# Loads of q, k and v issued in half-step portions behind TensorE's matmuls in a windowed-attention and mixture-of-experts kernel

## The chip, the cores and the metric

The kernel runs on one core of a Trainium2 chip. The metric is device time in microseconds (us) from the start to the end of one execution. The kernel before takes 690.67 us, the median of three runs that lie between 690.36 and 690.69.

The engines are named as the profile names them: PE is TensorE (matmuls), PEld its weight loads, DVE is VectorE, ACT is ScalarE, POOL is GpSimd, and SP is SyncE, which does no arithmetic here and issues transfers (DMAs). "SPq" is SP's instruction queue as the profile shows it. Each engine works through its own instructions in the order in which they were written; engines wait for each other and for transfers by semaphores.

## The reference

Two stages are chained. The first is an attention over 8 batches and 8 heads, with 512 local positions, 32 global positions and a head dimension of 64. The second is a mixture of experts (MoE) in which each token takes one of 8 experts, and may keep the expert of the token ahead of it.

```python
k_all = np.concatenate([k_g, k_l], axis=2)
v_all = np.concatenate([v_g, v_l], axis=2)
out_g = np.matmul(sm(scale * q_g @ k_all.T), v_all)          # global rows see all
mask = np.abs(pos[:, None] - pos[None, :]) <= 32             # local rows: a window
s_ll = np.where(mask, scale * q_l @ k_l.T, -1e9)
a_l = sm(np.concatenate([scale * q_l @ k_g.T, s_ll], axis=-1))
out_l = np.matmul(a_l, np.concatenate([v_g, v_l], axis=2))
x = concatenate([out_g, out_l]) as rows of 512, one per token (8 x 576)
...
logits = x @ w_gate;  local_gate = sigmoid(x @ w_local)
e = argmax(logits) if s == 0 or local_gate < 0.5 else prev_e  # sticky top-1
out = softmax(logits)[e] * (relu(x @ w1[e]) @ w2[e])
```

All of it is float32. The `.T` and `@` above shorten the reference's own `matmul` and `transpose` calls.

## The kernel before

**Stages.** The first third of the time is the attention (class `Attn`), the rest is the MoE. The change touches the attention alone, with the transfers that feed it and the one that takes its rows away.

**Units and steps.** Each batch has six units, in the order l0, l1, g0, l2, g1, l3. An l unit is a pair of heads for the local rows, a g unit is two pairs for the global rows. `run` goes over the 48 units in steps; step s belongs to batch b = s // 6 and has the place k = s % 6 in it. A step does the first part of its own unit (scores and the row maximum) and the second part (transposes, product with v, division) of the unit two steps earlier. An l unit is done in two halves, hb 0 and hb 1, of eight windows each.

In one step of an l unit PE therefore runs: transposes of the unit two steps back (`l_t`, L260), scores of the first half (`l_s`, mask L238 and products L243), one piece of a list of small follow-up work (`fpiece`), the product with v for the first half (`l_av`, L276), scores of the second half, another piece, and `l_av` of the second half. A step of a g unit runs `g_s` (L296) in place of the scores.

**The follow-up pieces** compute the gate for a batch that has ended: `f1` (L352, transposes of the batch's rows), `f1g`, `f2g` (L375), `f2` (L367, the gate's product) and `f3`. After `f3`, a generator `f3k` computes routing keys and probabilities on DVE in small portions (`drip`, called at fixed places between the other work), and ends with `f4`, the batch's store. So the store of batch b is written out during step k = 2 of batch b + 2, behind the DVE instruction at L771, which is the last to write into the rows.

**Buffers.** `raw` holds q and k of a pair, in a ring of four (528 KB each); `v` is a ring of five (1040 KB each); `qgb` a ring of two. A batch's output rows stand in `xa`, a ring of two (1056 KB each; 128 partitions by 4 row groups by 528 columns), and its global rows in `xg`, also a ring of two. Half hb of an l unit writes row groups 2 hb and 2 hb + 1 of `xa` (L284). Since the ring has two places, the first L284 of batch b + 2 can only write when the store of batch b has landed. In PSUM, `ps_s` has four banks for scores, `ps_t` two for transposes, and `ps_o` two, which `l_av`, `g_av`, `f2` and parts of `f3` take in turn: each needs the reader of the bank's earlier content to be done. The reader of an `l_av` bank is that half's chain on DVE, which ends with L284.

**Order.** The program is written under a manual schedule: each engine's queue holds the instructions in the order in which the Python code emits them. All loads and stores of this stage stand in SP's one queue, so that a DMA on SP which waits for a semaphore holds up every DMA behind it there. Besides its data waits, each DMA on SP waits for one of eight lanes (named DMAHW0 to DMAHW7 in the listing), that is for the landing of the DMA eight places ahead of it.

**Loads before the change.** At the head of each l step, `run` issues the qk load two pairs ahead (`load`, L178), with the global q at a batch's first pair (L182), and the v load one pair ahead (`loadv`, L188, one transfer of 1040 KB). The row store (L413) is one transfer of 1056 KB, followed by four small stores of the global rows (L417) and one of 32 rows of 16 columns (L418).

## Time and profile before

| What | Value |
|---|---|
| Median of three runs | 690.67 us (690.36 to 690.69) |
| The profiled execution | 694.06 us |
| Its span, first to last instruction | 692.3 us |
| PE busy | 670.5 us, 97% of the span |
| DVE busy | 426.2 us, 62% |
| ACT busy | 342.9 us, 50% |
| POOL busy | 207.7 us, 30% |
| Mean granted TensorE clock | 0.995 |
| Moved by DMA | 151.44 MB, mean 219 GB/s |

The profiled execution takes 1.76 us more than its span (694.06 - 692.3), which lies ahead of the first and behind the last instruction, and 3.39 us more than the median of the timed runs (694.06 - 690.67).

The profile is of one execution. Times in it count from the start of the span. A row of the timeline has the start, the time from there to the end of the last of a run of like instructions, the engine, the line, the operation, the output tile and the input tiles, and a count; in brackets stands the idle time of that engine just ahead of it, and what released it. A row of the waits has who waited for whom: the sum, the number of times, the longest. A row of the windows has the length of the stretch, then the busy time of PE, PEld, DVE, ACT and POOL with their instruction counts, the granted clock, the busy share of the DMA engines and what they moved in GB/s. Line numbers are those of the kernel before; those of the changed kernel are some 20 higher.

### The profile page before, as it was taken

The numbers are of one execution on the slowest core, as the hardware profiler recorded it, in microseconds if no ns is written. First come the engines' busy times: TensorE is split into PE (matmuls) and PEld (weight loads), VectorE is DVE, ScalarE is ACT, GpSimd is POOL, SyncE is SP. The second block draws the span as 40 slices with busy tenths as digits, with TensorE's granted clock in tenths as the row PEclk, the third lists the DMA queues.
The fourth block names the chain that finished last, engine by engine and source line by source line (L and its number), as shares of the span: only waits on it lengthen the run. The fifth ranks groups of instructions, "written<-read, shape, count | busy, mean of one in ns | idle before, by whom it ended". The sixth has DMA issues, their size and how long they took to land.

```text
span 692.3 us, 18408 instructions
## 1 busy us (share of the span) xinstructions
PE 670.5 (97%) x7253; PEld 561.1 (81%) x7253; DVE 426.2 (62%) x1050; ACT 342.9 (50%) x614; POOL 207.7 (30%) x342
## 2 busy tenths in 40 slices
PE   9999999999989899998998999999999999999995
PEld 7777777777767787897887988889898889888994
DVE  7878677688887777995517535335354516255572
ACT  4555556555455674653326625344444325255553
POOL 7634334343674301033013303040404020133023
PEclk9999999999999999999999999999999999999999
DMA  8956957866856497777418647337475417265673
GB/s 318 405 220 233 346 193 309 310 248 231 299 196 273 147 356 243 260 243 245 174 60 308 232 149 239 102 117 235 145 225 191 140 61 231 66 222 193 212 270 103
DMA packets 43011, 151.44 MB, mean 219 GB/s; under 512 B 7965, under 2 KB 9245, under 8 KB 38688
## 3 DMA queue, kind: packets, MB, share of 16 engines
q1 hardware_dynamic: 35536, 126.92, 51.6%
q0 software_dynamic: 6960, 21.90, 9.5%
q8 instruction: 77, 1.26, 0.7%
q14 instruction: 150, 1.23, 0.6%
q10 hardware_dynamic: 288, 0.13, 0.1%
HBM read 130.55 MB, written 19.69 MB: 217 GB/s over the span
## 4 chain that ended last, share of the span: by engine, by line
PE 60%; DVE 3%; issue 1%; ACT 0%; POOL 0%; POOLq 0%; DVEq 0%; ACTq 0%
PE ps L1267 29%; PE ps L1256 27%; PE ps L1210 3%; DVE wq L1165 1%; DVE wp L1165 1%; PE ps L1004 0%; PE ps L1379 0%; DVE xl L1165 0%; DVE xT L994 0%; POOL xa L1196 0%; DVE xT L996 0%; POOLq L1427 0%; DVE wp L1213 0%; PE ps L276 0%; DVE wq L1371 0%
## 5 line engine op out<-in xcount | busy, mean ns | idle before, releaser
L1273 POOL DMA_INDIRECT out_dram<-y,tk x39 | 40.4, 1036 | 317.6 <-ACT y L1272 246.3
L1267 PE MATMUL ps<-wp,wq 128*128 128x512 f32 x504 | 128.4, 402 | 1.0 <-ACT wq L1370 1.0
L1267 PEld LDWEIGHTS ps<-wp,wq 128*128 128x128 f32 x504 | 93.5, 190 | 21.1 <-ACT wq L1370 1.2
L1256 PE MATMUL ps<-wp,wp 128*128 128x256 f32 (+5 forms) x672 | 109.3, 322 | 0.2 <-issue 0.2
L1256 PEld LDWEIGHTS ps<-wp,wp 128*128 128x128 f32 x672 | 103.6, 188 | 5.3 <-issue 0.4
L1259 DVE SCALAR_TENSOR_TENSOR wq<-ps,wq 128x256 fp32r<-128x256 f32 (+5 forms) x80 | 41.7, 525 | 72.8 <-ACT wq L1258 62.6
L1213 DVE TENSOR_TENSOR wp<-ps,wp 128x512 fp32r<-128x512 f32 x40 | 27.5, 691 | 78.9 <-ACT wp L1212 78.8
L1258 ACT ACTIVATE wq<-ps 128x256 fp32r<-128x256 f32 (+5 forms) x80 | 37.3, 468 | 78.3 <-PE ps L1256 68.8
L191 POOL TENSOR_SCALAR_AFFINE_SELECT qbd<-raw 64x512 f32<-64x512 f32 x62 | 44.4, 716 | 103.3 <-PE ps L243 85.5
L243 PE MATMUL ps<-kx,qbd 128*64 128x128 f32 x1024 | 71.3, 280 | 0.2 <-issue 0.2
L1272 ACT ACTIVATE y<-ps,pp 128x512 f32<-128x512 f32 x39 | 26.9, 690 | 77.7 <-PE ps L1267 71.1
L243 PEld LDWEIGHTS ps<-kx,qbd 128*64 128x64 f32 x1024 | 55.1, 137 | 12.2 <-issue 7.8
L248 DVE TENSOR_REDUCE mx<-ps 128x4 f32<-128x512 f32 x64 | 43.9, 687 | 29.9 <-PE ps L243 29.9
L1165 DVE TENSOR_TENSOR wp<-raw,wp 128x1024 fp32r<-128x1024 f32 x47 | 57.0, 1217 | 2.8 <-ACT wp L1155 2.8
L254 ACT ACTIVATE pe<-pe 128x512 f32<-128x512 f32 x64 | 40.7, 637 | 31.7 <-DVE pe L250 31.7
L1196 POOL DMA_INDIRECT xa<-xs,idx x42 | 50.9, 1212 | 17.1 <-issue 9.4
L1155 ACT CAST wp<-raw 128x1024 fp32r<-128x1024 f32 x49 | 50.8, 1047 | 0.8 <-ACT hh L1258 0.5
L1212 ACT CAST wp<-ps 128x512 fp32r<-128x512 f32 x40 | 23.4, 590 | 53.9 <-PE ps L1210 53.3
L250 DVE TENSOR_TENSOR pe<-ps,mx 128x512 f32<-128x512 f32 x64 | 44.0, 688 | 1.6
L276 PEld LDWEIGHTS ps<-v,pt 128*32 128x32 f32 x2048 | 33.4, 110 | 13.1 <-issue 7.3
L276 PE MATMUL ps<-v,pt 128*32 128x65 f32 x2048 | 42.8, 222 | 1.1 <-issue 0.4
L262 ACT COPY pt<-ps 128x512 f32<-128x512 f32 x64 | 34.9, 610 | 17.6 <-PE ps L260 17.6
(280 smaller groups left out, 1183.3 us busy)
## 6 DMA issues: line engine op xcount, KB each, us to landing
raw<-in_w_dram SPq DMA_DIRECT2D x78, 512.0 KB, 4.1
v<-in_vw_dram SPq DMA_DIRECT2D x32, 1040.0 KB, 9.8
raw<-in_qk_dram SPq DMA_DIRECT2D x32, 528.0 KB, 8.2
xa<-in_w_dram SPq DMA_DIRECT2D x26, 512.0 KB, 5.2
xT<-in_w_dram SPq DMA_DIRECT2D x20, 512.0 KB, 3.5
xs<-xa SPq DMA_DIRECT2D x8, 1056.0 KB, 4.9
qgb<-in_qg_dram SPq DMA_DIRECT2D x8, 128.0 KB, 3.5
xa<-xs,idx POOLq DMA_INDIRECT x42
```

The source lines that it names most:

```text
L191: self.nc.gpsimd.affine_select(out=out, in_=in_, pattern=pat, compare_op=ALU.is_ge, fill=0.0, base=0, channel_multiplier=0)
L243: nc.tensor.matmul(sp[64 * t2:64 * t2 + 64, t], qbd[:, w], kf[:, f:f + P], start=False, stop=True, skip_group_check=True)
L248: nc.vector.tensor_reduce(out=mx, in_=st["sp"], axis=AX.X, op=ALU.max)
L250: nc.vector.tensor_tensor(out=st["pe"][:, 4 * hb:4 * hb + 4], in0=st["sp"], in1=mx.broadcast_to([P, 4, P]), op=ALU.subtract)
L254: self.nc.scalar.activation(out=pe, in_=pe, func=AF.Exp, scale=SCALE)
L276: nc.tensor.matmul(o[32 * w4:32 * w4 + 32, g, h], pt[:, 2 * g + w4 // 2, w4 % 2, h, :], v[:, w, h * (D + 1):(h + 1) * (D + 1)], start=True ...
L1155: nc.scalar.copy(out=hi, in_=raw)
L1165: (nc.gpsimd if pool else nc.vector).tensor_tensor(out=lo, in0=raw, in1=hi.bitcast(F32), op=ALU.subtract)
L1196: self.nc.gpsimd.indirect_dma_start(out=self.xr[j] if k == "early" else self.xr4[:, j], out_offset=None, in_=src, in_offset=bass.IndirectO ...
L1256: nc.tensor.matmul(ph, a[:, dc, fs], b_[:, dc, n0:n1], start=(n == 0), stop=(n == 11))
L1259: nc.vector.scalar_tensor_tensor(out=hl[:, fc, n0:n1], in0=ph, scalar=0.0, in1=hh[:, fc, n0:n1].bitcast(F32), op0=ALU.max, op1=ALU.subtract)
L1267: nc.tensor.matmul(py, a[:, fc, js], b_[:, fs], start=(fc == 0 and k == 0), stop=(fc == 7 and k == 2))
```

## The change

Three things are changed, all in `Attn`.

1. **A gate on each load.** `l_s`, `l_av`, `g_s` and `g_av` keep their last matmul in `self.gate`. Every load of q, k and v goes through the new function `get`, which adds to the DMA a dependency on the matmul that stands in `self.gate` when the load is written out. The loads ahead of the first step have none.
2. **v in two halves, and another place for the loads.** `loadv` has a parameter `hf` and moves 8 of a pair's 16 windows (520 KB). The loads no longer stand at the head of an l step: the new function `feed(s, hf)` is called twice in every step, once behind the scores (hf 0) and once at the step's end (hf 1). With k = 0, 1, 2 it issues the two halves of the v of pair 1 + k of this batch; with k = 3 qk of pair 0 of the next batch with the global q, then qk of pair 1; with k = 4 the halves of the next batch's v of pair 0; with k = 5 qk of pairs 2 and 3. In the first batch it also issues qk of pairs 2 and 3.
3. **The row store in two DMAs**, of row groups 0 and 1 and of 2 and 3 (528 KB each).

The diff:

```diff
--- before.py
+++ after.py
@@ -132,6 +132,7 @@
         self.low = 0
         self.banks = False
         self.npr = 0
+        self.gate = None
 
     def make_mask(self):
         nc, m0 = self.nc, self.m0
@@ -169,23 +170,45 @@
         yield
         nc.sync.dma_start(self.xs[0:P], zr)
 
+    def get(self, out, in_):
+        d = self.nc.sync.dma_start(out, in_)
+        if self.gate is not None:
+            self.tc.add_manual_dep(d.ins, self.gate.ins.name, mybir.DependencyInfo(mybir.DependencyClass.Sync, mybir.DependencyReason.DATA), reason="pace")
+
     def load(self, b, pr):
-        nc = self.nc
         if pr == 0:
             self.cur[b] = {"v": []}
         c = self.cur[b]
         t = c[("qk", pr)] = self.ld()
-        nc.sync.dma_start(t, self.qk[b, pr])
+        self.get(t, self.qk[b, pr])
 
     def load_g(self, b):
         g = self.cur[b]["qg"] = self.qgb()
-        self.nc.sync.dma_start(g, self.qg[b])
-
-    def loadv(self, b, pr):
-        nc = self.nc
-        v = self.v()
-        self.cur[b]["v"].append(v)
-        nc.sync.dma_start(v.rearrange("p w c -> p (w c)"), self.vw[b, pr])
+        self.get(g, self.qg[b])
+
+    def loadv(self, b, pr, hf):
+        vs = self.cur[b]["v"]
+        if hf == 0:
+            vs.append(self.v())
+        n = NW // 2 * VW
+        self.get(vs[pr].rearrange("p w c -> p (w c)")[:, n * hf:n * hf + n], self.vw[b, pr][:, n * hf:n * hf + n])
+
+    def feed(self, s, hf):
+        b, k = divmod(s, 6)
+        if k < 3:
+            if b == 0 and k < 2 and hf == 0:
+                self.load(0, 2 + k)
+            self.loadv(b, 1 + k, hf)
+            return
+        b += 1
+        if b == B:
+            return
+        if k == 4:
+            self.loadv(b, 0, hf)
+        else:
+            self.load(b, (k - 3) + hf)
+            if (k, hf) == (3, 0):
+                self.load_g(b)
 
     def cp(self, out, in_, pat):
         self.nc.gpsimd.affine_select(out=out, in_=in_, pattern=pat, compare_op=ALU.is_ge, fill=0.0, base=0, channel_multiplier=0)
@@ -240,7 +263,7 @@
             for t2 in range(2):
                 w = 8 * hb + 2 * t + t2
                 f = 32 * (3 * (w // 2) + w % 2)
-                nc.tensor.matmul(sp[64 * t2:64 * t2 + 64, t], qbd[:, w], kf[:, f:f + P], start=False, stop=True, skip_group_check=True)
+                self.gate = nc.tensor.matmul(sp[64 * t2:64 * t2 + 64, t], qbd[:, w], kf[:, f:f + P], start=False, stop=True, skip_group_check=True)
 
     def l_max(self, st, hb):
         nc = self.nc
@@ -273,7 +296,7 @@
             for h in range(2):
                 for w4 in range(4):
                     w = 8 * hb + 4 * g + w4
-                    nc.tensor.matmul(o[32 * w4:32 * w4 + 32, g, h], pt[:, 2 * g + w4 // 2, w4 % 2, h, :],
+                    self.gate = nc.tensor.matmul(o[32 * w4:32 * w4 + 32, g, h], pt[:, 2 * g + w4 // 2, w4 % 2, h, :],
                                      v[:, w, h * (D + 1):(h + 1) * (D + 1)], start=True, stop=True, skip_group_check=True)
         rs = self.rs()
         nc.vector.tensor_scalar(out=rs, in0=o[:, :, :, D:D + 1], scalar1=1e-9, scalar2=None, op0=ALU.add)
@@ -293,7 +316,7 @@
             for i in range(2):
                 pr = 2 * pp + i
                 k = c[("qk", pr)][:, SL:]
-                nc.tensor.matmul(sp[64 * i:64 * i + 64, 0:n1 - n0], c["qg"][:, pr], k[:, n0:n1], start=True, stop=True, skip_group_check=True)
+                self.gate = nc.tensor.matmul(sp[64 * i:64 * i + 64, 0:n1 - n0], c["qg"][:, pr], k[:, n0:n1], start=True, stop=True, skip_group_check=True)
             st["sp"].append(sp[:, 0:n1 - n0])
 
     def g_max(self, st):
@@ -336,7 +359,7 @@
         for ci, w in enumerate(GCH):
             for i in range(4):
                 pr, h = 2 * pp + i // 2, i % 2
-                nc.tensor.matmul(op[32 * i:32 * i + 32, 0:D + 1], st["pt"][:, ci, 32 * i:32 * i + 32],
+                self.gate = nc.tensor.matmul(op[32 * i:32 * i + 32, 0:D + 1], st["pt"][:, ci, 32 * i:32 * i + 32],
                                  c["v"][pr][:, w, h * (D + 1):(h + 1) * (D + 1)], start=(ci == 0), stop=(ci == 5), skip_group_check=True)
         rs = self.rsg()
         nc.vector.tensor_scalar(out=rs, in0=op[:, D:D + 1], scalar1=1e-9, scalar2=None, op0=ALU.add)
@@ -410,7 +433,8 @@
         hf, b4 = b // 4, b % 4
         rq = slice(32 * b4, 32 * b4 + 32)
         r0 = P * (1 + col(b))
-        nc.sync.dma_start(self.xs[r0:r0 + 4 * P].rearrange("(t p) r -> p t r", p=P), xa)
+        for t in range(0, 4, 2):
+            nc.sync.dma_start(self.xs[r0 + t * P:r0 + t * P + 2 * P].rearrange("(t p) r -> p t r", p=P), xa[:, t:t + 2])
         r0 = P * (1 + gcol(hf)) + 32 * b4
         xsg = self.xs[r0:r0 + 32]
         for h in range(4):
@@ -437,7 +461,8 @@
         for k in range(2):
             self.load(*pairs[k]["u"])
         self.load_g(0)
-        self.loadv(*pairs[0]["u"])
+        for hf in range(2):
+            self.loadv(0, 0, hf)
         self.cst.ident()
         warm = self.ps_o()[:, 0:P]
         for _ in range(8):
@@ -456,13 +481,6 @@
             sl = st is not None and st["k"] == "l"
             sg = st is not None and not sl
             if nl:
-                if npr + 2 < len(pairs):
-                    b, i = pairs[npr + 2]["u"]
-                    self.load(b, i)
-                    if i == 0:
-                        self.load_g(b)
-                if npr + 1 < len(pairs):
-                    self.loadv(*pairs[npr + 1]["u"])
                 npr += 1
                 if npr < len(pairs):
                     self.prep(pairs[npr])
@@ -480,6 +498,7 @@
             else:
                 self.g_s(nx)
                 self.g_max(nx)
+            self.feed(s, 0)
             fpiece()
             if sl:
                 self.l_av(st, 0)
@@ -494,6 +513,7 @@
                 self.l_av(st, 1)
             if sg:
                 self.g_av(st)
+            self.feed(s, 1)
             if nl:
                 if s in DEFER:
                     late = nx
```

The instructions on PE, DVE, ACT and POOL stand in the same order as before. What moves is SP's queue, and some waits. The piece of SP's queue around the store of batch 1, before the change; `raw`, `v` and `qgb` are loads, `xs<-xa` is the row store, `xs<-xg` and `xs<-gx` are the small stores, and a wait on PE_49 or DVE_49 is on an instruction of that engine:

```order
L178 DMA raw_80<-in_qk_dram 128x1056 [waits DMAHW2_49,Pool_49]
L188 DMA v_136<-in_vw_dram 128x2080 [waits DMAHW3_49,PE_49]
L413 DMA xs<-xa_109 128x4x528 [waits DMAHW4_49,DVE_49]
L417 DMA xs<-xg_111 32x2x64 [waits DMAHW5_49]
L417 DMA xs<-xg_111 32x2x64 [waits DMAHW6_49]
L417 DMA xs<-xg_111 32x2x64 [waits DMAHW7_49]
L417 DMA xs<-xg_111 32x2x64 [waits DMAHW0_49]
L418 DMA xs<-gx 32x16 [waits DMAHW1_49,DVE_49]
L178 DMA raw_77<-in_qk_dram 128x1056 [waits DMAHW2_49,PE_49,Pool_49]
L182 DMA qgb_152<-in_qg_dram 128x256 [waits DMAHW3_49]
L188 DMA v_132<-in_vw_dram 128x2080 [waits DMAHW4_49]
```

The same piece after the change (L174 is every load, L437 the row store, L441 and L442 the small stores):

```order
L174 DMA v_136<-in_vw_dram 128x1040 [waits DMAHW2_49,PE_49]
L174 DMA v_136<-in_vw_dram 128x1040 [waits DMAHW3_49,PE_49]
L174 DMA v_132<-in_vw_dram 128x1040 [waits DMAHW4_49,PE_49]
L437 DMA xs<-xa_109 128x2x528 [waits DMAHW5_49,DVE_49]
L437 DMA xs<-xa_109 128x2x528 [waits DMAHW6_49]
L441 DMA xs<-xg_111 32x2x64 [waits DMAHW7_49]
L441 DMA xs<-xg_111 32x2x64 [waits DMAHW0_49]
L441 DMA xs<-xg_111 32x2x64 [waits DMAHW1_49]
L441 DMA xs<-xg_111 32x2x64 [waits DMAHW2_49]
L442 DMA xs<-gx 32x16 [waits DMAHW3_49,DVE_49]
L174 DMA v_132<-in_vw_dram 128x1040 [waits DMAHW4_49,PE_49]
L174 DMA raw_77<-in_qk_dram 128x1056 [waits DMAHW5_49,PE_49,Pool_49]
```

The first half of the next pair's v (`v_132`) now stands ahead of the row store. It is written out by `feed(s, 0)` of step k = 2, so its wait on PE is for the last matmul of that step's `g_s`; before, the whole `v_132` stood behind the store.

On DVE, the first two writes of a batch into its `xa` buffer, the two halves of unit l0, before; L279 and L281 form the divisor and L284 writes the rows:

```order
L279 TENSOR_SCALAR rs1_122<-ps7_70 128x4 [waits PE_49]
L281 RECIPROCAL rs1_122<-rs1_122 128x4 [waits DVE_49]
L284 TENSOR_TENSOR xa0_108<-ps7_70,rs1_122 128x2x128 [waits DMAHW5_49,DVE_49]
L279 TENSOR_SCALAR rs2_123<-ps6_69 128x4 [waits PE_49]
L281 RECIPROCAL rs2_123<-rs2_123 128x4 [waits DVE_49]
L284 TENSOR_TENSOR xa0_108<-ps6_69,rs2_123 128x2x128 [waits DVE_49]
```

And after:

```order
L302 TENSOR_SCALAR rs1_122<-ps7_70 128x4 [waits PE_49]
L304 RECIPROCAL rs1_122<-rs1_122 128x4 [waits DVE_49]
L307 TENSOR_TENSOR xa0_108<-ps7_70,rs1_122 128x2x128 [waits DMAHW1_49,DVE_49]
L302 TENSOR_SCALAR rs2_123<-ps6_69 128x4 [waits PE_49]
L304 RECIPROCAL rs2_123<-rs2_123 128x4 [waits DVE_49]
L307 TENSOR_TENSOR xa0_108<-ps6_69,rs2_123 128x2x128 [waits DMAHW2_49,DVE_49]
```

Before, only the first of the two writes waits for a DMA, the whole store; now the first waits for one store and the second for the other.

## Prediction

> **What bounds the kernel now.** I read the page's busy times first, then the windows of the attention stage by batches, then the timeline of single steps, and last the waits of SP's queue.
>
> ```profile
> PE 670.5 (97%) x7253; PEld 561.1 (81%) x7253; DVE 426.2 (62%) x1050; ACT 342.9 (50%) x614; POOL 207.7 (30%) x342
> ```
>
> PE is busy for 97% of the span. For the stage that is changed, the windows from one batch's start to the next (at PE's L359, which comes once in a batch) say more:
>
> ```profile
> 34.30:62.59 28.29, 28.11 (x590) 21.27 (x588) 21.22 (x75) 16.03 (x38) 11.06 (x25) 1.00 0.63 237
> 62.59:90.89 28.30, 27.89 (x589) 21.29 (x587) 21.30 (x72) 16.01 (x38) 11.06 (x25) 1.00 0.75 275
> 90.89:118.67 27.78, 27.78 (x589) 21.18 (x587) 21.13 (x72) 16.00 (x38) 11.05 (x25) 1.00 0.76 281
> 118.67:146.45 27.78, 27.78 (x589) 21.16 (x587) 21.15 (x72) 16.01 (x38) 11.06 (x25) 1.00 0.77 280
> ```
>
> Two of the four batches take 27.78 us and PE is busy for all of it, at full granted clock; DVE, the next, has 21. Loads and stores cost these two batches nothing. The other two take 0.51 and 0.52 more (28.29 - 27.78, 28.30 - 27.78). The two places:
>
> ```profile
> 36.08 0.87 PE L243 MATMUL ps<-kx,qbd 128*64 128x128 f32 x11 [0.17 <-issue]
> 84.05 0.27 PE L276 MATMUL ps<-v,pt 128*32 128x65 f32 x2 [0.41 <-issue]
> ```
>
> Both are "issue": PE waited for nothing that the profile shows. So smoother loading has at most 1.03 us to win here, and that only if these gaps have to do with DMA traffic. With PE full, whatever now makes PE wait in a batch is added to the end.
>
> **What the change removes, adds and moves.** *The splits.* 32 v loads become 64 and 8 row stores become 16, 40 more DMAs on SP. An issue costs SP some 0.4 us (rows at 91.77 and 96.21 below), so 5 more per batch are 2 us of SP's time; SP does nothing else, and in the piece of timeline below it is idle for most of a batch. Price 0; it would count only where something urgent stands behind them, which is the next point. *The gates on PE.* A gate needs a signal from a matmul that PE executes anyway, and eight more separate semaphore instructions; the like of them stand in the trace:
>
> ```profile
> L359 PEldq EVENT_SEMAPHORE  x7: 51/51/51, 33.7 to 208.2; - x7
> ```
>
> Eight by 0.051 is 0.41 us at most; PEld has 6 us of room in a batch, so I take 0.
>
> *The row store.* This is the term that I forecast by. SP before, around the store of batch 1:
>
> ```profile
> 91.77 0.38 SPq L413 DMA_DIRECT2D xs<-xa  x1
> 92.19 3.91 SPq L417 DMA_DIRECT2D xs<-xg  x4
> 96.21 0.37 SPq L418 DMA_DIRECT2D xs<-gx  x1
> 96.71 1.44 SPq L178 DMA_DIRECT2D raw<-in_qk_dram  x1
> ```
>
> The store is issued right behind what it waits for, the last write of the rows:
>
> ```profile
> 91.66 0.08 DVE L771 MEMSET xa<- 128x28 f32 x1
> SPq L413 <- DVE xa L771: 48.0, 5, 11.3
> ```
>
> After the change a half of the next v stands ahead of it in the queue, and waits for the last matmul of `g_s` in step k = 2 (L296). The timeline of PE and DVE over the same time:
>
> ```profile
> 94.61 1.14 PE L296 MATMUL ps<-raw,qgb 128*64 128x256 f32 x8
> 95.67 0.27 PE L375 MATMUL ps<-xgT,wgg 128*32 128x32 f32 x8
> 97.33 0.42 DVE L284 TENSOR_TENSOR xa<-ps,rs 128x256 f32<-128x256 f32 x1 [0.42 <-DMA xs<-xa]
> 98.07 0.42 DVE L284 TENSOR_TENSOR xa<-ps,rs 128x256 f32<-128x256 f32 x1
> 99.67 1.06 PE L367 MATMUL ps<-xT,wgl 128*32 128x512 f32 x8
> 100.55 0.64 PE L276 MATMUL ps<-v,pt 128*32 128x65 f32 x32
> ```
>
> L296 is over at about 95.7. The v half then takes SP to about 96.2, and the first half of the store is issued there, the second at 96.65: 4.4 us and 4.9 us later than 91.77. Who waits for it: DVE's first L284 of batch b + 2 already now waits 0.42 us for the store's landing (in the store after that 1.12, below). After the change the first L284 waits for store half 0 and the second for half 1. Behind L284 on DVE stand the maxima of the next scores, and behind DVE stands PE: `f2` (L367, at 99.67) needs the PSUM bank that the first L284 reads, and the next `l_av` (L276, at 100.55) the bank of the second. Before, these two L284 end at 97.75 and 98.49, so PE has about 2 us of cover. The second L284 may start no later than 100.13 (100.55 - 0.42); what it starts later, PE loses.
>
> How long the landing takes. The waits of DVE give it for two stores: 97.33 - 91.77 = 5.56 us, and for the store at 119.55 the row below gives 125.81 - 119.55 = 6.26. The other two, at 63.46 and 147.33, were not waited for, so took less than 5.17 (68.63 - 63.46; 152.50 - 147.33).
>
> ```profile
> 63.46 0.38 SPq L413 DMA_DIRECT2D xs<-xa  x1
> 68.63 0.42 DVE L284 TENSOR_TENSOR xa<-ps,rs 128x256 f32<-128x256 f32 x1
> 119.55 0.38 SPq L413 DMA_DIRECT2D xs<-xa  x1
> 125.81 0.42 DVE L284 TENSOR_TENSOR xa<-ps,rs 128x256 f32<-128x256 f32 x1 [1.12 <-DMA xs<-xa]
> 147.33 0.38 SPq L413 DMA_DIRECT2D xs<-xa  x1
> 152.50 0.42 DVE L284 TENSOR_TENSOR xa<-ps,rs 128x256 f32<-128x256 f32 x1
> DMA to landing us min/median/max: 4.7/4.9/6.7
> ```
>
> The last row is that of L413, all eight. I take 5.2, between the median 4.9 and 5.56, for both halves together: they move the same bytes. Ahead of them now stands the v half, 520 KB (0.53 MB). At the rate of a stretch in which loads run alone and the DMA engines are full, it is 0.53 MB / 386 GB/s = 1.4 us:
>
> ```profile
> 104.00:106.00 2.00, 2.00 (x18) 1.25 (x17) 1.92 (x10) 1.39 (x3) 1.34 (x5) 1.00 1.01 386
> ```
>
> The store is issued 0.45 behind the v half, so it is pushed by 1.4 - 0.45 = 0.95 if the transfers are served in turn. No row shows that; the bounds are 0 and 1.4, and I take 0.95 because both go over the same 16 engines. [...]
>
> So the second half lands at 96.2 + 5.2 + 0.95 = 102.35, L284 ends at 102.77, and PE starts L276 at 102.77 instead of 100.55: **2.2 us** per batch. It falls on batches b + 2 = 2 to 5, four times, where the store is issued ahead of the gate. That of batch 4 is issued later in its batch, at 166.39, where the last gate ahead of it in the new order, the first half's scores in that step, has opened at about 165.5; the ones behind it lie likewise, so I charge them nothing.
>
> ```profile
> 164.50 1.09 PE L243 MATMUL ps<-kx,qbd 128*64 128x128 f32 x16
> 166.39 0.38 SPq L413 DMA_DIRECT2D xs<-xa  x1
> ```
>
> Sum: 4 x 2.22 = 8.9; less 1.03 for the issue gaps, which I take as gone since the loads in lumps go: +7.8 (rounded). The profiled execution took 694.06 (692.3 span and 1.76 around it), so 701.9; that execution is 3.39 above the median of the runs, so the forecast for the median is 690.67 + 7.8 = **698.5**.
>
> Its bounds: low, a landing of 4.7 and nothing for the v half: 96.2 + 4.7 + 0.42 - 100.55 = 0.77, by four 3.1, less 1.03: 692.7. High, 6.26 and 1.4: 3.73, by four 14.9, the gaps staying: 705.6.
>
> *The loads.* They are issued later: qk of the next batch's pair 0 waits for its gate (99.67), but stands behind the four small stores, 3.9 us, which now begin near 97.1; so at about 101.9, where before it was 96.71. The cover:
>
> ```profile
> 102.52 1.50 POOL L191 TENSOR_SCALAR_AFFINE_SELECT qbd<-raw 64x512 f32<-64x512 f32 x2 [6.48 <-PE ps L243]
> 104.08 1.33 POOL L191 TENSOR_SCALAR_AFFINE_SELECT kx<-raw 128x128 f32<-128x128 f32 x4
> 112.81 0.88 PE L243 MATMUL ps<-kx,qbd 128*64 128x128 f32 x12
> raw<-in_qk_dram SPq DMA_DIRECT2D x32, 528.0 KB, 8.2
> v<-in_vw_dram SPq DMA_DIRECT2D x32, 1040.0 KB, 9.8
> ```
>
> POOL rearranges it at 102.52, before PE uses it at 112.81 (115.0 with the delay). Even with the old median landing of 8.2 it is there at 110.1, and POOL's 2.9 us end at 113.0: POOL waits, PE does not. The v halves have two steps from gate to use, and a step is 27.78 / 6 = 4.6 us. So 0; if the cover were gone, each microsecond would be one of PE.
>
> At the end of the stage SP's first weight loads of the MoE stand behind the last gated loads, some 3 us later:
>
> ```profile
> 213.63 26.11 SPq L1145 DMA_DIRECT2D raw<-in_w_dram  x6
> 227.57 1.05 ACT L1155 CAST wp<-raw 128x1024 fp32r<-128x1024 f32 x1
> ```
>
> ACT uses the first 13.9 us after its issue, so 3 us less cost nothing.
>
> **Rivals.** *1. The store lands in time, faster.* A half of the store is half the bytes. The least time that a small store took, 1.5 us (row below), plus half of what the whole takes beyond it, (4.9 - 1.5) / 2 = 1.7, is 3.2 us; if the halves and the v half are served side by side, half 1 lands at 96.65 + 3.2 = 99.85, ahead of 100.13, and PE waits for nothing. If the issue gaps then go with the lumps in the loads, it is 690.67 - 1.03 = **689.6**. It decides from a landing of half 1 within 3.48 us of its issue.
>
> ```profile
> DMA to landing us min/median/max: 1.5/1.5/1.5
> ```
>
> (That is L418, 32 rows of 16 columns.) For it speaks that two halves can be waited for apart; against it that they share the engines with each other and that no whole store landed in under 4.7. [...]
>
> *2. Late by a little, no change.* Half 1 lands at about 100.4, between the two cases: 0.25 us of PE by four is 1.0, and the issue gaps pay for it: **690.7**. For it: the wait starts on DVE, which has 6 us of room in a batch. Here belongs also that the gates do not pace anything and the store isn't held, with nothing gained; against that stands the order of SP's queue.
>
> *3. The loads come late as well.* If a qk load in the new place takes over 10.2 us to land (115.0 - 2.9 - 101.9), PE waits for POOL too. At 2 us in each of seven batches it is 14 us more than the forecast, **712**. For it speaks that the four loads of a batch now share the time with the late store; against it, that lumps of 1040 KB ahead of a qk load are what made 8.2.
>
> **How the numbers follow.** Chances: the forecast 0.73, rival 1 0.09, rival 2 0.13, rival 3 0.05. A measurement of this kernel can tell 0.2% (1.4 us) from no change. Faster is rival 1: 0.09. Same is rival 2: 0.13. Slower is the forecast and rival 3: 0.78. The range for 8 in 10 goes from 690.9, with the upper part of rival 2 in it, to 704.5, the forecast's high bound with the gaps gone; the forecast's own bounds are 692.7 and 705.6.
>
> **What would show it.** In the profile after: the first half of the row store issued about 0.5 us behind the end of L296's matmuls in batches 2 to 5, and not behind L771; a wait of DVE on `xs<-xa` four times, of 2 to 5 us; PE idle by some 2 us ahead of L367 and L276 there, put down to DVE; windows of about 30 us for batches 2 to 5 and 27.8 for the others; the two issue gaps smaller. It would be wrong if DVE waits for the store and PE does not, if PE waits ahead of L243 for POOL, if windows of the first batches stay at 28.3, or if the store's second half lands within 3.5 us of its issue.

## The result, and the profile after

| | Median | Range | Runs |
|---|---|---|---|
| Before | 690.68 us | 690.36 to 691.48 | 4 |
| Changed | 713.01 us | 711.78 to 714.01 | 4 |

The changed kernel takes 1.0321 times as long as the kernel before (95% interval 1.0301 to 1.0340), 22.3 us more. I had forecast +7.8 us, 698.5, with a range up to 704.5: the sign was right, the size was not. The profiled execution of the changed kernel took 711.78 us, 17.7 more than that of the kernel before, which was 3.4 above its median.

The busy times on the page of the changed kernel:

```profile
PE 675.0 (95%) x7253; PEld 562.7 (79%) x7253; DVE 423.4 (60%) x1050; ACT 343.4 (48%) x614; POOL 209.8 (30%) x342
```

PE executes the same 7253 matmuls and is busy 4.5 us longer (675.0 - 670.5); the rest of the loss is idle time. The windows from batch to batch, again from L382 (the old L359) to L382, tell where:

```profile
35.71:63.49 27.78, 27.78 (x589) 21.17 (x587) 21.50 (x75) 16.00 (x38) 11.03 (x25) 1.00 0.78 236
63.49:96.16 32.67, 29.15 (x589) 21.66 (x588) 21.02 (x72) 16.09 (x38) 11.05 (x25) 0.95 0.76 236
96.16:129.17 33.01, 29.47 (x589) 22.18 (x587) 20.93 (x72) 16.08 (x38) 11.03 (x25) 0.95 0.77 239
129.17:162.92 33.75, 30.12 (x590) 22.38 (x588) 20.77 (x72) 16.09 (x38) 11.07 (x25) 0.90 0.74 230
162.92:197.64 34.72, 31.16 (x614) 23.14 (x612) 23.67 (x78) 16.27 (x38) 11.16 (x25) 0.95 0.79 249
```

The last of these batches took 30.01 before, of which PE was busy 29.65:

```profile
146.46:176.47 30.01, 29.65 (x614) 22.70 (x612) 23.66 (x78) 16.20 (x38) 10.35 (x23) 1.00 0.67 240
```

The first window is free of loss, 0.51 better than before. Batches 2 to 5, the next four, take 134.15 us instead of 113.88: 20.3 us more. In each, PE is idle for some 3.5 us (32.67 - 29.15, and so on; 14.3 in the four), and is busy for longer than before with the same work (29.15 instead of 27.78; 6.9 us in the four), at a granted clock of 0.90 to 0.95 in place of 1.00. The two make 21.2; the four windows of before had 0.9 us of such time already. The other differences between the two profiles are 1.4 us lost ahead of the first window (35.71 - 34.30; the larger part is an "issue" gap of 0.88 us at 18.32) and some gains later, among them one stretch at a lowered clock that only the profile of before has (shown further below).

The waits named in the expectation are there:

```profile
DVE xa L307 <- DMA xs<-xa: 26.1, 8, 6.0
PE ps L390 <- DVE xa L307: 13.5, 4, 3.6
```

DVE waits 26.1 us for the row store, where it was 1.5, and PE waits four times for DVE, ahead of f2 (L390, the old L367). One of the four, in the timelines of SP, DVE and PE:

```profile
64.25 0.08 DVE L791 MEMSET xa<- 128x28 f32 x1
67.20 1.14 PE L319 MATMUL ps<-raw,qgb 128*64 128x256 f32 x8
68.38 0.33 SPq L174 DMA_DIRECT2D v<-in_vw_dram  x1
68.80 0.90 SPq L437 DMA_DIRECT2D xs<-xa  x2
75.37 0.42 DVE L307 TENSOR_TENSOR xa<-ps,rs 128x256 f32<-128x256 f32 x1 [5.90 <-DMA xs<-xa]
76.79 0.42 DVE L307 TENSOR_TENSOR xa<-ps,rs 128x256 f32<-128x256 f32 x1 [0.71 <-DMA xs<-xa]
71.24 1.09 PE L266 MATMUL ps<-kx,qbd 128*64 128x128 f32 x16
75.85 1.94 PE L390 MATMUL ps<-xT,wgl 128*32 128x512 f32 x8 [3.52 <-DVE xa L307]
77.56 1.09 PE L299 MATMUL ps<-v,pt 128*32 128x65 f32 x32
```

The last write of the rows starts at 64.25 and takes 0.08 us. The v half ahead of the store goes out at 68.38, when L319 is over; the two halves of the store at 68.80 and some 0.45 later. Half 0 has landed at 75.37 (6.6 us after its issue), half 1 at 76.79 (7.5 us). PE stands for 3.52 us, and then runs f2 in 1.94 us where it took 1.06, and the next `l_av` in 1.09 where it took 0.64.

### The profile page after: what moved, and what is told of

The parts are those of the page before. It is cut to its first block, busy times and chain, and to the rows that moved or that the text cites. A ratio compares the mean times of both kernels' runs of the same rounds, so it can differ in the third digit from the quotient of the medians.

```text
span 710.1 us, 18507 instructions
## 1 busy us (share of the span) xinstructions
PE 675.0 (95%) x7253; PEld 562.7 (79%) x7253; DVE 423.4 (60%) x1050; ACT 343.4 (48%) x614; POOL 209.8 (30%) x342
## 3 DMA queue, kind: packets, MB, share of 16 engines
q14 instruction: 151, 1.24, 0.6%
## 4 chain that ended last, share of the span: by engine, by line
PE 54%; DVE 6%; issue 1%; ACT 1%; POOL 0%; POOLq 0%; DVEq 0%; ACTq 0%
PE ps L1287 26%; PE ps L1276 24%; PE ps L1230 2%; DVE wp L1185 2%; DVE wq L1185 1%; DVE hl L1279 1%; PE ps L1399 1%; DVE xT L1014 0%; DVE xT L1016 0%; POOL xa L1216 0%; DVE o L930 0%; DVE xl L1233 0%; PE ps L1024 0%; POOLq L1447 0%; DVE wp L1233 0%
## 5 line engine op out<-in xcount | busy, mean ns | idle before, releaser
L266 PE MATMUL ps<-kx,qbd 128*64 128x128 f32 x1024 | 72.8, 286 | 0.6 <-POOL kx L214 0.6
L266 PEld LDWEIGHTS ps<-kx,qbd 128*64 128x64 f32 x1024 | 56.6, 140 | 12.6 <-issue 8.0
L271 DVE TENSOR_REDUCE mx<-ps 128x4 f32<-128x512 f32 x64 | 43.8, 684 | 27.5 <-PE ps L266 27.4
L1216 POOL DMA_INDIRECT xa<-xs,idx x42 | 52.5, 1250 | 17.3 <-issue 9.7
L299 PEld LDWEIGHTS ps<-v,pt 128*32 128x32 f32 x2048 | 34.6, 113 | 16.3 <-issue 12.1
L299 PE MATMUL ps<-v,pt 128*32 128x65 f32 x2048 | 44.4, 228 | 2.1 <-issue 1.3
L214 POOL TENSOR_SCALAR_AFFINE_SELECT kx<-raw 128x384 f32<-128x384 f32 (+3 forms) x127 | 42.6, 368 | 3.0 <-DMA raw<-in_qk_dram 0.8
```

The costliest lines, as they stand in the source:

```text
L214: self.nc.gpsimd.affine_select(out=out, in_=in_, pattern=pat, compare_op=ALU.is_ge, fill=0.0, base=0, channel_multiplier=0)
L266: self.gate = nc.tensor.matmul(sp[64 * t2:64 * t2 + 64, t], qbd[:, w], kf[:, f:f + P], start=False, stop=True, skip_group_check=True)
L271: nc.vector.tensor_reduce(out=mx, in_=st["sp"], axis=AX.X, op=ALU.max)
L299: self.gate = nc.tensor.matmul(o[32 * w4:32 * w4 + 32, g, h], pt[:, 2 * g + w4 // 2, w4 % 2, h, :], v[:, w, h * (D + 1):(h + 1) * (D + 1)] ...
L1216: self.nc.gpsimd.indirect_dma_start(out=self.xr[j] if k == "early" else self.xr4[:, j], out_offset=None, in_=src, in_offset=bass.IndirectO ...
```

## Experiments

Theory A is the prediction's: SP's queue holds the row store behind a gated load, DVE waits for the late landing, and PE waits for DVE. Theory B puts the loss on the loads: gates, halves or new places by themselves. Each group was timed beside its own runs of the kernel before, so times are compared within a group.

| Run | Time | Before beside it | Ratio (95% interval) | Difference |
|---|---|---|---|---|
| e1, v half of k = 2 behind the store | 707.60 | 695.65 | 1.0189 (1.0143 to 1.0235) | +12.0 |
| e2, store not held | 695.69 | 695.65 | 1.0006 (0.9994 to 1.0019) | 0.0 |
| e3, store on ACT's queue | 717.50 | 695.65 | 1.0329 (1.0282 to 1.0375) | +21.9 |
| e4, before, with the store held | 705.37 | 695.65 | 1.0139 (1.0116 to 1.0163) | +9.7 |
| a0, the changed kernel again | 718.60 | 695.44 | 1.0345 (1.0313 to 1.0377) | +23.2 |
| e5, third row buffer, first form | 743.36 | 695.44 | 1.0694 (1.0653 to 1.0736) | +47.9 |
| e6, filler matmuls | 711.10 | 695.44 | 1.0237 (1.0205 to 1.0268) | +15.7 |
| e7, whole store | 722.89 | 695.44 | 1.0392 (1.0355 to 1.0429) | +27.5 |
| e5b, third row buffer | 692.42 | 691.98 | 1.0005 (0.9990 to 1.0021) | +0.4 |
| e8, no gates | 693.19 | 691.98 | 1.0022 (1.0012 to 1.0032) | +1.2 |
| e9, two-part store alone | 692.81 | 691.98 | 1.0016 (0.9998 to 1.0034) | +0.8 |
| e10, store held, v half behind it | 698.59 | 691.98 | 1.0098 (1.0073 to 1.0123) | +6.6 |

### Moving the loads behind the store

e1:

```diff
-            self.feed(s, 0)
+            if s % 6 != 2:
+                self.feed(s, 0)
...
+            if s % 6 == 2:
+                self.feed(s, 0)
             self.feed(s, 1)
```

> The changed kernel, but in each step k = 2 both halves of v are issued at the step's end, behind the row store; one gated half (of step k = 1, hf 1) still stands ahead of the store. Theory A (the store is held in SP's queue by a gated load, and PE pays): the store goes out about 2.05 us earlier (its gate opens at 66.3 instead of 68.4), so PE's idle time ahead of f2 falls from 3.5 to about 1.5 us in four batches: 713.0 - 4 x 2.05 = 704.8, and down to 698 if PE's clock is no longer lowered after the shorter idle time. Theory B (the halves or the gates themselves cost the time, by late loads or slow small transfers): no change, 710 to 714.

e2, which also takes the last gated load of step k = 1 from ahead of the store:

```diff
-            self.feed(s, 0)
+            if s % 6 != 2:
+                self.feed(s, 0)
...
-            self.feed(s, 1)
+            if s % 6 == 2:
+                self.feed(s - 1, 1)
+                self.feed(s, 0)
+            if s % 6 != 1:
+                self.feed(s, 1)
```

> As the run before, but the second half of step k = 1 is issued behind the row store too, so that the store waits only for its own data. All gates, halves and the two-part store stay. Theory A: the store goes out at L791's end as before the change, DVE waits under 1 us, PE not at all: 690 to 693. Theory B: 708 to 714.

e1 came out at +12.0, inside what theory A expected (+7 to +14 when its 698 and 704.8 are taken against 690.7): PE's waits ahead of f2 fell to 1.4 to 1.6 us. e2 has no loss at all. Its timeline and the window of the same batch:

```profile
63.29 0.90 SPq L437 DMA_DIRECT2D xs<-xa  x2
69.53 0.42 DVE L307 TENSOR_TENSOR xa<-ps,rs 128x256 f32<-128x256 f32 x1 [1.13 <-DMA xs<-xa]
62.42:90.06 27.64, 27.64 (x590) 21.20 (x588) 21.18 (x72) 15.99 (x38) 11.08 (x25) 1.00 0.86 281
```

The store goes out at 63.29, 0.9 us into the batch instead of 5.3 (68.80 - 63.49); DVE waits for 1.13 us and PE is busy for the whole of its batch. All gates, all halves and the two-part store are still in this kernel. So theory B falls: with the order of SP's queue mended at this place, the whole loss is gone.

### Another queue for the store

```diff
-            nc.sync.dma_start(self.xs[r0 + t * P:r0 + t * P + 2 * P]...
+            nc.scalar.dma_start(self.xs[r0 + t * P:r0 + t * P + 2 * P]...
```

> The changed kernel with the two halves of the row store issued from ACT's queue instead of SP's; everything else as in the changed kernel, so the gated v halves keep their places on SP. Theory A: 690 to 694, since nothing on SP holds the store. If the v halves delay it through the shared transfer engines rather than through the order of SP's queue: still some 2 us late in four batches, 698 to 704. Theory B: 708 to 714.

It came out at +21.9. Taken against 690.7 as above, that is not theory A's range nor that of the shared engines (+7 to +13); by the number alone it lies where theory B was put (+17 to +23). The rows show another reason than B's. ACT's queue at the store, and DVE:

```profile
66.34 1.07 ACT L285 COPY pt<-ps 128x512 f32<-128x512 f32 x2 [1.24 <-PE ps L283]
66.83 1.16 ACTq L437 DMA_DIRECT2D xs<-xa  x2
72.63 0.42 DVE L307 TENSOR_TENSOR xa<-ps,rs 128x256 f32<-128x256 f32 x1 [3.74 <-DMA xs<-xa]
75.03 0.42 DVE L307 TENSOR_TENSOR xa<-ps,rs 128x256 f32<-128x256 f32 x1 [1.70 <-DMA xs<-xa]
```

On ACT the store stands behind the copies L285, which wait for PE's transposes, here for 1.24 us. It is issued at 66.83, 0.49 behind the start of the copies, in a batch that starts at 62.91, so 3.9 us into it, and its halves take 5.8 us and over 7 us, beside the v halves. The run doesn't tell the order of SP's queue from the sharing of the transfer engines, as I had meant it to; it moved the store from one late place to another.

### The store held in the kernel before

```diff
...                                        # g_s keeps its last matmul in self.gate
-        nc.sync.dma_start(self.xs[r0:r0 + 4 * P]..., xa)
+        d = nc.sync.dma_start(self.xs[r0:r0 + 4 * P]..., xa)
+        if b < 4:
+            self.tc.add_manual_dep(d.ins, self.gate.ins.name, ...)    # last matmul of g_s
```

> The kernel before, with one edit: the row store of batches 0 to 3 (one transfer) waits for the last matmul of g_s in step k = 2, with no v half ahead of it and all loads in their old places. Theory A: the store is issued at about 95.75 instead of 91.77 and lands 5.2 later; PE loses 0.8 us in four batches, 694, and up to 701 if the clock is lowered after it. Theory B: 690.7, no change.

One wait, on four DMAs, makes +9.7 us, at the upper end of what theory A gave, with no gate on a load and all loads in their old order. (Those behind the store go out some 4 us later too, the next qk at 71.86 of a batch that starts at 62.69, where it was 67.75 of 62.59; PE waits for none of them.) The first of the four:

```profile
67.58 0.38 SPq L414 DMA_DIRECT2D xs<-xa  x1
72.09 0.42 DVE L285 TENSOR_TENSOR xa<-ps,rs 128x256 f32<-128x256 f32 x1 [3.42 <-DMA xs<-xa]
```

The whole store, issued 4.9 us into its batch (67.58 - 62.69), lands in 4.5 us; in the other three batches, with nothing right ahead of it either, it takes 6.7, 5.0 and 6.0. PE's waits ahead of f2 are 1.03, 3.23, 1.50 and 2.47 us, and the granted clock was lowered at the second and the fourth: 0.95 in the windows of these two batches, 1.00 in the other two.

### The changed kernel again, and its row buffers, store and clock

> The changed kernel as it is, on the chip of the next three runs, as their point of comparison: 3.0 to 3.4% above the kernel before (21 to 23 us).

a0 is the changed kernel, unaltered, for the next three runs: +23.2.

e5 gives the ring of batch rows a third buffer, and takes the room from v:

```diff
-NV = 5
+NV = 4
...
+        self.xa.t.append(at1.tile([P, 4, ROW], F32, name="xa2", tag="xa2"))
```

> The changed kernel with a third buffer in the ring of batch rows (and four instead of five v buffers, for the room). The row store is as late as in the changed kernel, but its buffer is now needed again a batch later. Theory A (the cost is DVE's wait for the late store, and PE's behind it): all of the loss in batches 2 to 5 goes, within 2 us of the kernel before (-1 to +2). Theory B (gates, halves and late loads cost the time themselves): still 15 to 22 us above the kernel before.

Its +47.9 us answers another question. With four v buffers, the load of the next batch's first v in step k = 4 takes the buffer that `g_av` of the same step still has to read, so `g_av` waits for that load and multiplies with the next batch's v: part of the computation is changed, and a wait is added that the theory isn't about.

```profile
PE ps L363 <- DMA v<-in_vw_dram: 33.5, 7, 7.2
```

e5b mends it by issuing that load behind `g_av`:

```diff
-            self.feed(s, 0)
+            if s % 6 != 4:
+                self.feed(s, 0)
...
+            if s % 6 == 4:
+                self.feed(s, 0)
             self.feed(s, 1)
```

> The changed kernel with a third buffer in the ring of batch rows, four v buffers for the room, and both halves of the next batch's first v at the end of step k = 4 (behind the last reader of the buffer that they take). The row store is held as late as in the changed kernel; only nobody waits for it. Theory A (the cost is the wait of DVE for the late store, with PE's wait and its lowered clock behind it): within -1 to +2 us of the kernel before. Theory B (the gates and halves cost the time themselves): still 15 to 22 us above.

It came out at +0.4. The store is still held by the gate and its landing median is 6.1 us; but no engine of this stage waits for it, and PE is busy all through the same batch:

```profile
DMA to landing us min/median/max: 2.8/6.1/8.7
63.01:90.64 27.63, 27.63 (x589) 21.20 (x587) 21.00 (x72) 15.97 (x38) 10.98 (x25) 1.00 0.86 280
```

So the late store costs only through the buffer that it keeps (+0.4 us with a third one, +23.2 in a0 without). e6 fills PE's wait:

```diff
+        if 1 <= b <= 4:
+            fl = self.bank(self.ps_t)
+            for i in range(12):
+                nc.tensor.matmul(fl[:, i % 4], self.cst.idf, self.cst.idf, start=True, stop=True, ...)
         gp = self.ps_o()
```

> The changed kernel with 12 matmuls that nobody reads (128 by 128, 0.27 us each, 3.3 us) put ahead of f2 in the four batches where PE waits there, so that PE is busy in nearly all of its wait. Theory A with a lowered clock as the second part: the idle time as a whole stays covered by the filler, so the time lost is what is left of the wait, and the slower matmuls after it (1.4 to 2.3 us per batch, 7 in all) go: 14 to 16 us above the kernel before instead of 21 to 23. If the clock has nothing to do with it: 21 to 24 above.

```profile
70.89 2.94 PE L391 MATMUL ps<-idf 128*128 128x128 f32 x24
62.12:93.77 31.65, 30.79 (x614) 23.86 (x612) 20.96 (x72) 16.09 (x38) 10.95 (x25) 1.00 0.79 243
62.76:95.26 32.50, 29.00 (x590) 21.68 (x588) 20.75 (x72) 16.12 (x38) 11.10 (x25) 0.95 0.76 239
75.77 0.67 PE L299 MATMUL ps<-v,pt 128*32 128x65 f32 x32 [0.53 <-DVE xa L307]
```

The second row is e6's batch, the third the same batch of a0. Useless work makes the kernel 7.5 us faster (718.6 to 711.1), and it lands at +15.7, within the +14 to +16 expected with the lowered clock. In e6's batch the granted clock is 1.00, and its own work takes 27.85 us of PE (30.79 - 2.94), where a0 needs 29.00. Over the four batches the two profiles differ by 3.7 us; the rest of the 7.5 lies in the MoE, where the profile of a0 has two slow stretches of the clock and that of e6 none, so I count only the 3.7 as shown for this stage, and the place inside the expected interval is partly luck. 3.7 is less than the 6.7 us that the clock adds to PE's busy time in a0 there (worked out like the 6.9 above). The reason is in the last row, of e6: with f2 at full clock, PE comes to the next `l_av` ahead of half 1 of the store and waits there, 0.53, 0.35, 1.42 and 0.57 us in the four batches, 2.9 in all.

e7 makes the store one transfer again:

```diff
-        for t in range(0, 4, 2):
-            nc.sync.dma_start(self.xs[r0 + t * P:r0 + t * P + 2 * P]..., xa[:, t:t + 2])
+        nc.sync.dma_start(self.xs[r0:r0 + 4 * P]..., xa)
```

> The changed kernel with the row store as one transfer again; gates and v halves stay. If the split makes the store slow (smaller transfers): faster than the changed kernel, by up to 6 us. If bytes and place set the landing (theory A): the first write waits for the whole store instead of its half, so f2 starts 1.0 to 1.4 us later per batch and the next l_av about as before; 0 to 4 us above the changed kernel.

It is 4.3 us slower than a0 (722.89 - 718.60), just past the end of theory A's interval: the first write then waits for the whole store, and PE's four waits ahead of f2 add up to more.

```profile
PE ps L390 <- DVE xa L307: 20.6, 4, 5.6
```

The split of the store, which I had charged nothing, saves about 1 us per batch here.

### Gates, the split, and the v half ahead

e8 takes the gates off the changed kernel, e9 puts the two-part store into the kernel before and nothing else:

```diff
-        if self.gate is not None:
+        if False:
             self.tc.add_manual_dep(d.ins, self.gate.ins.name, ...)
```

> The changed kernel without the dependencies on matmuls: halves, places of the loads and the two-part store stay, and a load waits only for its buffer and its lane. Theory A: the v half ahead of the store no longer holds it, so 0 to +3 us against the kernel before. If the places of the loads or the halves are the cause: 10 us or more above.

> The kernel before with the row store in two transfers and nothing else changed. Theory A: the store is issued on time; both parts land by about 97.4 in the batch that starts at 90.9, and no engine on the path waits: -0.5 to +0.5 us against the kernel before.

e8 is at +1.2 and e9 at +0.8, whose interval includes no change; both are nearly free, as theory A has it. e9 is a little over the 0.5 that I had given it, within what this group's runs of one kernel differ.

e10 settles what the v half ahead of the store adds: it moves the half behind the store, as e1 does, and lets the store itself wait for the matmul that the half waited for.

```diff
...                                        # g_s keeps its last matmul in self.gs
-            nc.sync.dma_start(self.xs[r0 + t * P:r0 + t * P + 2 * P]..., xa[:, t:t + 2])
+            d = nc.sync.dma_start(self.xs[r0 + t * P:r0 + t * P + 2 * P]..., xa[:, t:t + 2])
+            if b < 4:
+                self.tc.add_manual_dep(d.ins, self.gs.ins.name, ...)    # last matmul of g_s
...
-            self.feed(s, 0)
+            if s % 6 != 2:
+                self.feed(s, 0)
...
+            if s % 6 == 2:
+                self.feed(s, 0)
```

> As the run in which both v halves of step k = 2 stand behind the row store, but the store itself waits for the same matmul of g_s as the v half ahead of it did in the changed kernel. So it is issued as late as there (0.4 us sooner) with no v half right ahead in the transfer queues. If the wait for the gate alone makes the cost: about the changed kernel, 20 to 22 us above the kernel before. If the v half ahead adds to the landing, as I charged with 0.95 us, or more: its landing falls from some 6.5 and 7.5 us to 4.7 to 5.5, PE's wait by 1.5 to 2.5 us per batch and the lowered clock with it: 8 to 14 us above.

It came out at +6.6, below the 8 to 14 of its second case. SP, DVE, PE and the windows of batches 2 and 3:

```profile
69.05 0.90 SPq L437 DMA_DIRECT2D xs<-xa  x2
72.92 0.42 DVE L307 TENSOR_TENSOR xa<-ps,rs 128x256 f32<-128x256 f32 x1 [2.78 <-DMA xs<-xa]
74.36 0.42 DVE L307 TENSOR_TENSOR xa<-ps,rs 128x256 f32<-128x256 f32 x1 [0.73 <-DMA xs<-xa]
73.40 1.06 PE L390 MATMUL ps<-xT,wgl 128*32 128x512 f32 x8 [0.40 <-DVE xa L307]
74.88 0.67 PE L299 MATMUL ps<-v,pt 128*32 128x65 f32 x32 [0.42 <-issue]
64.16:93.03 28.87, 28.05 (x589) 21.11 (x587) 20.89 (x72) 16.08 (x38) 11.04 (x25) 1.00 0.81 268
93.03:123.15 30.12, 27.91 (x590) 21.12 (x588) 21.12 (x72) 16.09 (x38) 11.07 (x25) 1.00 0.81 260
```

PE is idle for 0.8 us in the one and 2.2 in the other, and the clock stays at 1.00, as it does in batches 4 and 5. So the late issue alone costs 6.6 us, and the v half ahead of the store makes the rest of the 22 to 23 that the changed kernel loses. What the transfer queue does about the store, in the changed kernel and in e10, each over the stretch from 68 to 77 us (the first row has what the DMA engines moved in 40 slices of 0.225 us; the others are the store's median landing there). The changed kernel:

```profile
GB/s 222 333 333 462 370 204 111 148 74 55 18 148 166 277 296 351 324 371 374 385 412 413 432 375 413 422 413 385 403 349 216 145 32 103 93 158 143 227 240 425
xs<-xa SPq DMA_DIRECT2D x2, 528.0 KB, 7.0
```

e10:

```profile
xs<-xa SPq DMA_DIRECT2D x2, 528.0 KB, 4.3
```

In the changed kernel, slices 9 to 11 (69.8 to 70.5) move 74, 55 and 18 GB/s: the earlier load has run out, the v half issued at 68.38 hasn't begun in earnest, and the store issued at 68.80 isn't moving, though the engines are busy for only 0.7, 0.4 and 0.1 of these slices. In the packet records the v half's packets come thickly only from about 70.6, 2.2 us after its issue. The first packet of the store is at 71.76, 2.96 us after its issue (2.6 to 3.0 in the four batches); in e10 it is at 69.95 and in the kernel before at 64.38, each 0.9 us after the issue, as for all stores of batches 2 to 5 of these two. So this store began 2.0 us later with the v half issued ahead of it (2.96 - 0.9), and 1.2 us behind the time from which the v half's packets come thickly (71.76 - 70.6).

## Why the prediction was right and wrong, step by step

**Right: what bounds the stage, and the mechanism.** The store goes out behind the v half at the end of L319 (predicted 0.5 us behind, measured 68.80 against 68.34), in batches 2 to 5 and no others; DVE waits for it at the first two writes of the rows, PE for DVE. e2, e4 and e5b show each link by itself: the place in SP's queue, the wait alone, the buffer.

**Wrong: "the store is ... pushed by 1.4 - 0.45 = 0.95".** The step let the store's issue overlap the transfer of the v half, as if that began with its issue and the two were served in turn; the 0.95 was my estimate from the rate of 386 GB/s, and no run shows it. The landing of half 1 came 7.99 us after the first issue (76.79 - 68.80), where 6.15 was predicted (5.2 + 0.95); over the four batches it is 7.6 to 8.4, 7.9 on average. With the half behind the store, in e10, it is 5.31 (74.36 - 69.05), and 5.3 to 6.7, 5.9 on average, over the four; half 0 lands after 4.4 on average instead of 6.4. So the v half ahead costs 2.0 us, not 0.95, nearly all of it in the later first packet, and the store by itself takes 0.7 more than the 5.2. Without that half, in e10, PE's idle time adds up to 5.9 us in the four batches, between the low bound (3.1) and the forecast (8.9).

**Wrong by the size that follows: "4 x 2.22 = 8.9".** PE's idle time is 14.3 us in the four batches, 3.6 each, near the high bound of 3.73 that I had worked out.

**Missing: the price of the idle time on PE's clock.** No term had it, and it is 6.9 us of busy time; e6 shows that 3.7 of such a sum is gained when the clock stays up, the rest being covered by the wait for half 1. The windows right at the wait:

```profile
72.00:75.25 3.25, 0.33 (x8) 0.09 (x2) 0.00 (x0) 0.39 (x1) 0.00 (x0) 1.00 0.98 364
75.25:78.66 3.41, 2.81 (x41) 1.30 (x41) 2.38 (x6) 0.68 (x2) 0.00 (x0) 0.50 0.86 280
78.66:82.00 3.34, 3.34 (x63) 2.61 (x65) 2.63 (x10) 0.88 (x2) 1.31 (x2) 1.00 0.24 87
```

From 75.25, 0.6 us before PE's wait of 3.52 is over, the granted clock is 0.50 for 3.41 us, then 1.00 again. I had read the clock of 1.00 in the four windows of before as a given; PE is idle in each of them for 0.41 us at most (28.30 - 27.89). The profile of before even has such a stretch, behind three waits in the MoE (0.77, 1.08 and 0.97 us):

```profile
378.56:381.97 3.41, 2.95 (x7) 2.38 (x8) 1.48 (x2) 0.00 (x0) 0.00 (x0) 0.50 0.88 310
```

The forecast's wait of 2.2 us is shorter than those that had a lowered clock every time, 3.08 to 3.63 us, and the high bound's 3.73 is longer; one of 2.47 us had it in e4, and one of 2.21 in the kernel before had not (last section). So another rival was due: the same wait, and in each batch where the clock is lowered up to 1.7 us more, half of the 3.41 us at 0.50. In e6, where PE is kept busy through most of the wait, the granted clock is 1.00 in all four batches.

**Not as forecast: which instruction waits.** I expected PE to lose its time ahead of L299, by half 1. It loses it ahead of f2, by half 0: half 0 lands so late that f2 becomes the later of the two, and half 1 is hidden behind a slow f2; e6, with a fast f2, waits for both.

**Issue gaps.** They went where I said in the first window (28.29 to 27.78), but one of 0.88 us came up at 18.32. They don't go with the loads in lumps: e9, with the loads of before, has neither of the two, and e8, with the halves but no gates, has both again (0.27 us at 36.01, 0.57 at 84.14). The gain of 1.03 wasn't one.

**Right: the loads.** PE waits 0.6 us in all for POOL's rearranged k, and nowhere for v:

```profile
L266 PE MATMUL ps<-kx,qbd 128*64 128x128 f32 x1024 | 72.8, 286 | 0.6 <-POOL kx L214 0.6
```

The rivals fell: the store doesn't land in time, no batch is only a little late, and the loads cost PE nothing more than that. That rival 3's 712 lies close to the measured 713 is chance.

Neither the change nor any of its parts beat the kernel before by more than the measurement tells.

## What to carry to other kernels

A load that waits for compute is a gate for whatever stands behind it in an issue queue that is worked through in order: here the store went out 4.5 us behind the end of its data (68.80 against 64.33). Before pacing loads so, list the stores behind them and ask when their buffers are needed again. Charge a transfer behind another with its later first packet, and not with the other's bytes alone: here 2.0 us where I had charged 0.95. And where PE is full, price a new wait of a few microseconds with the clock that may be lowered at it, here about half as much again (6.9 us of busy time on 14.3 of idle time).

## What the runs showed of the hardware

- At PE's waits the granted clock was lowered to 0.50 in stretches of 3.41 us: in the changed kernel from 75.25, 109.39 and 174.24, and for twice that, 6.83 us, from 140.11; in the kernel before from 378.56 (each has one more in the last 4 us of its span). Waits of 3.08 to 3.63 us had such a stretch every time, one of 2.47 in e4 too, and so had two waits of 1.36 and 1.39 us with 1 us of work between them, in e3, 1.64 and 0.68 in e1, and the 0.77, 1.08 and 0.97 of the kernel before; another pair in e3 (1.24 and 1.45) had not, nor had single waits of 2.21 us in the kernel before, of 1.83 in the changed kernel (ahead of L1230, at 337.67), and of 1.77 (e10) or less.

- The longest wait doesn't separate the two kinds (1.08 us with a lowered clock and 2.21 without, both in the kernel before), nor does the sum of a pair (2.32 with it in e1, 2.69 without in e3). No run varied the length of a wait alone, so what decides stays open. The wait of 2.21 us with the stretch behind it, in the kernel before, and one of the cases with 3.23 us, in e4:

```profile
318.43 0.66 PE L1210 MATMUL ps<-idf,xa 128*128 128x128 f32 x4 [2.21 <-DVE wp L1213]
318.43:321.84 3.41, 3.41 (x37) 2.91 (x38) 2.19 (x6) 1.86 (x3) 0.00 (x0) 1.00 0.31 119
101.00:104.20 3.20, 0.03 (x4) 0.03 (x4) 0.49 (x2) 0.00 (x0) 0.00 (x0) 1.00 0.49 121
104.20:107.60 3.40, 3.40 (x45) 1.70 (x47) 2.39 (x7) 1.11 (x2) 0.00 (x0) 0.50 0.92 333
```

- A few last packets ended a transfer over a microsecond behind the others: of the 512 packets of the store of the batch at 63.49, 498 (97%) were through by 75.0, and the last 14 ended one by one, 0.08 us apart, from 75.07 to 76.14. DVE's wait for half 1 ended at 76.79, 0.65 us behind the last of them. In e4 95% of each store's packets are through 3.7 to 3.9 us after its issue in all four batches, and the last one after 4.1, 6.1, 4.4 and 5.3 us: this tail orders PE's waits of 1.03, 3.23, 1.50 and 2.47 us. What held those packets back stays open.
